# All scales of an attention and two-layer gated kernel from one product with a constant matrix

## The chip, the cores and the metric

The kernel runs on one core of a Trainium2 chip. The metric is the device time of one execution in microseconds (us); three executions of the kernel before gave 1435.85, 1441.42 and 1451.26 us, median 1441.42 us. Engines are named PE (TensorE matmul), PEld (its weight loads), DVE (VectorE), ACT (ScalarE), POOL (GpSimd) and SP (SyncE, which issues the DMAs here).

## What is computed

Attention with queries pooled by two over 32 heads (batch 4, 8 heads, 1152 keys, head width 64), then two feed-forward layers on 2304 tokens of width 512 with 2048 hidden columns, the first gated by a cosine, the second by a sigmoid:

```
q_pool = q.reshape(B, H, S // 2, 2, D).mean(axis=3)
attn   = softmax(q_pool @ k.T / sqrt(D));  x = attn @ v          # 2304 x 512
h = x @ w_in1;  x = (h * cos(h)) @ w_out1
h = x @ w_in2;  out = (h / (1 + exp(-h))) @ w_out2
```

q, k, v are 32-bit; the four weight matrices arrive as 64-bit floats.

## The kernel before

**Split numbers.** Every matmul operand is written as a sum of two 16-bit numbers, high and low, after multiplication by a power of two, and three products (high·high, high·low, low·high) give the result. The power of two comes from the largest magnitude of the operand, over all 128 partitions. A tile's maximum per partition is one DVE reduction; the helpers `scale_steps_` and `mean_scales` make of it a scale `s` and its inverse `u` that all partitions hold.

**scale_steps_ (lines 87 to 120)** serves the weight pieces (16 per layer, `wide`), the eight blocks of x, the rest block (`mrem`) and the nine blocks of y: 50 calls. It transposes the 128 maxima into one row (L91, PE, tile `mt`), reduces that row on one partition (L94, DVE, `mxw` or `mxx`), masks the exponent there (L98 and L101 for the weights, L105 otherwise), clamps it (L107, `pbw` or `pbx`), spreads it over all partitions by a product with `ones` (L113, PE, `bc`), and forms `s` and `u` (L117, L120). `mt` and `bc` take two turns of one rotating PSUM tag, which the first layer's `h` tiles use too.

**mean_scales (lines 122 to 137)** serves the 16 head pairs of the attention: one product of the maxima with a constant 128x128 matrix `mean` of 2^-7 (L127, `bm`) and three DVE steps (L130, L131, L135). The power of two then follows the mean of the maxima and not the largest of them.

**Stages.** Head pairs are processed in nine tiles each, 144 in all: scores (`sp`, L419), their evacuation with the maximum (`sc`, L438), exponential (L446), split (L452, POOL L457), a DMA transposition (`hlT`), the product with v (`pv`, L470). During the first batch the weights of layer 1 are decoded from 64-bit beside it (`weight_steps`: ACT L235, DVE L236, L239, L244, L247, then a scale, then ACT L267, L268 and POOL L269). From the second batch on the units of layer 1 run beside the attention (`h`, L550; `y`, L610; the cosine on DVE L575, L576, L585, L590). After the last tile the rest of layer 1 runs with the decoding of layer 2's weights, whose staging holds six half pieces; then layer 2 runs on PE alone (`h`, L550; `o`, L631) in nine blocks, each of which makes the scale of the next one (`y_split`).

**What sets the order.** Each engine executes its instructions in program order. The program is written as generators with priorities (`early`, `ahead`), and a scheduler turns them into the order of each engine before the launch: a step that becomes ready earlier in its model is placed earlier, and everything around it moves as well. SP issues all DMAs, in its own order.

Of the kernel before, what the change touches and what calls it, by code (L numbers as in the profile page):

```python
# [11 lines left out]
F32 = mybir.dt.float32  # L12
F16 = mybir.dt.float16
I32 = mybir.dt.int32
AF = mybir.ActivationFunctionType
ALU = mybir.AluOpType
AX = mybir.AxisListType
# [27 lines left out]
def attention_moe_moe_kernel(ctx, tc, q, k, v, w_in1, w_out1, w_in2, w_out2, out):  # L45
# [22 lines left out]
    ident = const.tile([128, 128], F32, name="ident")  # L68
    ones = const.tile([4, 128], F32, name="ones")
# [3 lines left out]
    def make_consts(pool):  # L73
        nc.vector.memset(ones, 1.0)
        nc.vector.memset(mean, 2.0**-7)
        nc.vector.memset(halfpi, math.pi / 2)
        io = pool.tile([128, 128], I32, name="io", tag="kn", bufs=NB_N)
        nc.gpsimd.iota(io, pattern=[[1, 128]], base=0, channel_multiplier=-1)
        nc.vector.tensor_scalar(out=ident, in0=io, scalar1=0, scalar2=None, op0=ALU.is_equal)
# [4 lines left out]
    def scale_steps(*a):  # L84
        return early(scale_steps_(*a), P_CH)

    def scale_steps_(m, n, pool, res, tag, wide=False):


        mt = pool.tile([128, 2, GW], F32, tag="h", name="mt")[:, 0, 0:128]  # L90
        nc.tensor.transpose(mt[0:n, :], m, ident)  # L91
        yield
        mx = small.tile([4, 1], F32, name="mx" + tag, tag="mx" + tag)
        nc.vector.tensor_reduce(out=mx[0:n], in_=mt[0:n, :], axis=AX.X, op=ALU.max)  # L94
        pb = small.tile([4, 1], F32, name="pb" + tag, tag="pb" + tag)
        mi, pi = mx.bitcast(I32)[0:n], pb.bitcast(I32)[0:n]
        if wide:
            nc.vector.tensor_scalar(  # L98
                out=pi, in0=mi, scalar1=3, scalar2=0x3F800000, op0=ALU.logical_shift_left, op1=ALU.bitwise_and
            )  # L100
            nc.vector.scalar_tensor_tensor(  # L101
                out=pi, in0=mi, scalar=1 << 30, in1=pi, op0=ALU.bitwise_and, op1=ALU.bitwise_or
            )
        else:
            nc.vector.tensor_scalar(out=pi, in0=mi, scalar1=EXP_MASK, scalar2=None, op0=ALU.bitwise_and)  # L105
        pb = pb[0:n]
        nc.vector.tensor_scalar(out=pb, in0=pb, scalar1=TINY, scalar2=2.0**-12, op0=ALU.max, op1=ALU.mult)  # L107
        dg = pb
        if n > 1:
            dg = small.tile([4, 4], F32, name="dg" + tag, tag="dg" + tag)[0:n, 0:n]  # L110
            nc.vector.tensor_scalar(out=dg, in0=ident[0:n, 0:n], scalar1=pb, scalar2=None, op0=ALU.mult)
        bc = pool.tile([128, 2, GW], F32, tag="h", name="bc")[:, 0, 0:4]
        nc.tensor.matmul(bc[:, 0:n], ones[0:n, :], dg, start=True, stop=True)  # L113
        yield

        s, u = res
        nc.vector.tensor_scalar(  # L117
            out=s.bitcast(I32), in0=bc.bitcast(I32)[:, 0:n], scalar1=EXP_MASK, scalar2=None, op0=ALU.bitwise_xor
        )
        nc.vector.tensor_scalar(out=u, in0=bc[:, 0:n], scalar1=0.5, scalar2=None, op0=ALU.mult)  # L120

    def mean_scales(m, n, pool, res):

        bc = pool.tile([128, 2, GW], F32, tag="h", name="bm")[:, 0, 0:4]
        nc.tensor.matmul(bc[:, 0:n], mean, m, start=True, stop=True)  # L127
        yield
        s, u = res
        nc.vector.tensor_scalar(out=u, in0=bc[:, 0:n], scalar1=TINY, scalar2=2.0**-3, op0=ALU.max, op1=ALU.mult)  # L130
        nc.vector.tensor_scalar(  # L131
            out=s.bitcast(I32), in0=u.bitcast(I32), scalar1=EXP_MASK, scalar2=EXP_MASK,
            op0=ALU.bitwise_and, op1=ALU.bitwise_xor,
        )
        nc.vector.tensor_scalar(  # L135
            out=u.bitcast(I32), in0=u.bitcast(I32), scalar1=EXP_MASK, scalar2=None, op0=ALU.bitwise_and
        )
# [20 lines left out]
    def run_all(g):  # L158
        for _ in g:
            pass  # L160
# [23 lines left out]
    def weight_steps(w, srcs, stage, pspool, eng, nsub, bufs, ahead):  # L184
# [35 lines left out]
        def decode(kind, p):  # L220
# [35 lines left out]
            for _ in scale_steps(m1, 1, pspool(), (s, u), "w", wide):  # L256
                pass
# [3 lines left out]
        def write(kind, p):  # L261
# [10 lines left out]
            if (kind, p) == ("i", npc - 1):  # L272

                nc.vector.tensor_reduce(out=w.kg, in_=w.si, axis=AX.X, op=ALU.min)
                nc.vector.tensor_reduce(out=w.ug, in_=w.ui, axis=AX.X, op=ALU.max)
                nc.vector.tensor_scalar(out=w.kg, in0=w.kg, scalar1=2.0**-22, scalar2=None, op0=ALU.mult)
                nc.vector.tensor_scalar(out=w.ug, in0=w.ug, scalar1=2.0**22, scalar2=None, op0=ALU.mult)
# [63 lines left out]
    def pair_prep(at, P):  # L341
# [19 lines left out]
        yield from early(mean_scales(m3, 3, ps_h, (s, u)), P_CH)  # L361
# [142 lines left out]
    def x_scale_consts(w, s, u, first):  # L504
# [12 lines left out]
            out=c.a, in0=w.ui, scalar1=u, scalar2=1.0 / two_pi if first else 1.0, op0=ALU.mult, op1=ALU.mult  # L517
# [4 lines left out]
    def x_split(at, mp, x32, i, blk, w):  # L522
# [6 lines left out]
        yield from scale_steps(m, 1, ps_h, (s, u), "x")  # L529
# [118 lines left out]
    if True:  # L648
# [10 lines left out]
        make_consts(at.src)  # L659
# [202 lines left out]
        run_all(scale_steps(mrem, 1, ps_h, (srem, urem), "x"))  # L862
# [34 lines left out]
        def y_split(yb):  # L897
# [5 lines left out]
            yield from scale_steps(m, 1, ps_m, (yb.s, yb.u), "x")  # L903
# [99 lines left out]
```

## Time and profile before

| quantity | value |
|---|---|
| median of three executions | 1441.42 us |
| profiled execution, time | 1445.72 us |
| profiled execution, span | 1444.0 us |
| PE busy | 1190.0 us, 82% |
| DVE busy | 1026.4 us, 71% |
| ACT busy | 783.1 us, 54% |
| POOL busy | 578.5 us, 40% |

The span runs from the first instruction to the last; 1.7 us of the time lie around it. Busy shares are averages over stages with different limits, so the stage windows below matter more than this table: 0 to 250 us is the first batch with the decoding of layer 1's weights, 250 to 880 us the other three batches beside layer 1, 880 to 1056 us the rest of layer 1 with layer 2's weights, and from 1056 us on layer 2. Instructions overlap a little at their ends, so the distance from one start to the next is the time that an instruction takes from its engine, and the duration printed beside it is longer.

### The profile page before, as it was taken

The page shows a single profiled execution, that of the slowest core. Times are in us where ns is not written, and L with a number is a line of the kernel's source. Part 1 is how long each engine was busy: PE and PEld are TensorE (multiplying, and loading weights), DVE is VectorE, ACT ScalarE, POOL GpSimd, SP SyncE. Part 2 cuts the span into 40 slices and gives each one's busy share as a digit, 9 for nine tenths or more (in the row PEclk, how much of TensorE's full clock was granted, in tenths as well). Part 3 has the DMA queues.
Part 4 walks back from the last instruction along what each step waited for, and adds up shares of the span by engine and source line. Part 5 has one row for each costly group of instructions (what it writes and reads, how often), then busy time and mean ns, then how long its engine had stood idle before and what let it go on. Part 6 is the DMA issues. An engine that isn't in the chain of part 4 may idle for free. (4 is left out here: it accounts for less than half of the span.)

```text
span 1444.0 us, 25499 instructions
## 1 busy us (share of the span) xinstructions
PE 1190.0 (82%) x10070; PEld 860.8 (60%) x10070; DVE 1026.4 (71%) x2110; ACT 783.1 (54%) x1001; POOL 578.5 (40%) x329
## 2 busy tenths in 40 slices
PE   1664644787988579898888979888899999999998
PEld 0343423565776356666666667777776666666665
DVE  7999998689887788896899895989962222333212
ACT  3876867568786587775687773645631111111110
POOL 1576755446577365663566451464420000000000
PEclk9976757898999799998999999999999999999999
DMA  8799998959799799978899964323310000000001
GB/s 255 149 242 206 233 213 150 173 126 167 154 204 193 135 208 197 194 136 164 137 192 204 176 150 86 117 94 116 112 59 30 1 30 30 30 30 15 15 1 30
DMA packets 493592, 186.22 MB, mean 129 GB/s; under 512 B 433568, under 2 KB 468384, under 8 KB 493472
## 3 DMA queue, kind: packets, MB, share of 16 engines
q1 hardware_dynamic: 493472, 184.59, 61.0%
q8 instruction: 79, 1.29, 0.4%
q14 instruction: 41, 0.34, 0.1%
HBM read 66.58 MB, written 9.44 MB: 53 GB/s over the span
## 5 line engine op out<-in xcount | busy, mean ns | idle before, releaser
L457 POOL TENSOR_TENSOR hl<-sc,hl 128x1152 f16<-128x1152 f32 x144 | 367.5, 2561 | 218.1 <-ACT hl L452 138.1
L419 PE MATMUL sp<-kT,qT 128*128 128x512 f16 (+1 forms) x768 | 198.0, 377 | 109.1 <-DVE sc L438 80.1
L550 PEld LDWEIGHTS <-ih 128*128 128x128 f16 x2304 | 227.4, 100 | 77.9 <-issue 19.2
L438 DVE TENSOR_SCALAR_CACHE_REDUCE sc<-sp,psu 128x512 f32<-128x512 f32 (+1 forms) x288 | 229.6, 805 | 50.7 <-PE sp L419 47.4
L563 ACT ACTIVATE hk<-h,ca 128x512 f32<-128x512 f32 x144 | 98.1, 682 | 303.9 <-PE h L550 302.6
L470 PE MATMUL pv<-vt,hlT 128*128 128x130 f16 (+1 forms) x1440 | 192.8, 239 | 56.0 <-DMA hlT<-hl 42.7
L446 ACT ACTIVATE sc<-sc,nb 128x1152 f32<-128x1152 f32 x144 | 179.9, 1250 | 94.4 <-DVE nb L443 74.6
L550 PE MATMUL h<-ys,ih 128*128 128x256 f16 x1152 | 200.3, 275 | 3.1 <-ACT hk L563 3.1
L470 PEld LDWEIGHTS <-hlT 128*128 128x128 f16 (+1 forms) x1440 | 146.7, 111 | 91.0 <-DMA hlT<-hl 54.7
L550 PE MATMUL h<-xT,ih 128*128 128x256 f16 x1024 | 190.5, 282 | 9.8 <-DMA xT<-xn 5.5
L474 PE MATMUL pv<-vt,hlT 128*128 128x65 f16 (+1 forms) x1440 | 185.0, 209 | 0.0
L452 ACT ACTIVATE hl<-sc 128x1152 f16<-128x1152 f32 x144 | 165.4, 1156 | 28.0 <-DMA hlT<-hl 23.0
L419 PEld LDWEIGHTS <-qT 128*128 128x128 f16 x768 | 76.4, 108 | 174.1 <-issue 135.7
L598 DVE TENSOR_SCALAR gh<-hk,ck 128x1024 f16<-128x1024 f32 x36 | 27.0, 750 | 193.7 <-PE o L631 187.7
L610 PE MATMUL y<-gh,oh 128*128 128x256 f16 x576 | 160.5, 279 | 3.5 <-ACT y L619 2.7
L610 PE MATMUL y<-gl,oh 128*128 128x256 f16 x576 | 160.5, 279 | 0.6 <-POOL gl L591 0.6
L610 PE MATMUL y<-gh,ol 128*128 128x256 f16 x576 | 160.4, 279 | 0.0
L550 PE MATMUL h<-ys,il 128*128 128x256 f16 x576 | 158.2, 275 | 0.0
L474 PEld LDWEIGHTS <-hlT 128*128 128x128 f16 (+1 forms) x1440 | 143.3, 109 | 19.0 <-issue 10.7
L550 PE MATMUL h<-xT,il 128*128 128x256 f16 x512 | 144.0, 281 | 0.0
L591 POOL TENSOR_TENSOR gl<-tt,gh 128x1024 f16<-128x1024 f32 x36 | 89.6, 2489 | 98.1 <-DVE gh L590 90.3
L610 PEld LDWEIGHTS <-oh 128*128 128x128 f16 x1152 | 113.0, 100 | 22.8 <-issue 4.8
(291 smaller groups left out, 2143.3 us busy)
## 6 DMA issues: line engine op xcount, KB each, us to landing
wst<-in_moe_w_in_dram SPq DMA_DIRECT2D x32, 512.0 KB, 4.7
wst<-in_moe_w_out_dram SPq DMA_DIRECT2D x32, 512.0 KB, 4.3
stk<-in_k_dram SPq DMA_DIRECT2D x32, 288.0 KB, 3.9
stv<-in_v_dram SPq DMA_DIRECT2D x32, 288.0 KB, 4.4
stq<-in_q_dram SPq DMA_DIRECT2D x32, 256.0 KB, 3.1
ydr<-y SPq DMA_DIRECT2D x9, 512.0 KB, 3.6
y32b<-ydr SPq DMA_DIRECT2D x9, 512.0 KB, 3.9
out_dram<-osb SPq DMA_DIRECT2D x16, 256.0 KB, 3.4
```

What stands on the lines that cost most here:

```text
L419: nc.tensor.matmul(sp[:, o - a:o - a + n], P.qT[e][:, t, :], kT[:, o:o + n], start=(e == 0), stop=(e == 1))
L438: nc.vector.tensor_scalar(out=T.sc[:, a:z], in0=sp, scalar1=T.P.su, scalar2=None, op0=ALU.mult, op1=ALU.min, accum_out=mx[:, x:x + 1],)
L446: nc.scalar.activation(out=T.sc, in_=T.sc, func=AF.Exp, scale=-1.0, bias=nb)
L452: nc.scalar.activation(out=hi, in_=T.sc, func=AF.Copy)
L457: nc.gpsimd.tensor_tensor(out=T.hl[:, 1, :], in0=T.sc, in1=T.hl[:, 0, :], op=ALU.subtract)
L470: nc.tensor.matmul(G.pv[r, T.gi], T.hlT[:, 0, c, r], P.vt[i][:, c], start=(c == 0), stop=(c == KC - 1), skip_group_check=True,)
L474: nc.tensor.matmul(G.pv[r, T.gi, 0], T.hlT[:, 1, c, r], P.vt[i][:, c, 0], start=False, stop=(c == KC - 1), skip_group_check=True,)
L550: nc.tensor.matmul(hp, wt[:, c, f * 128:(f + 1) * 128], xt(c), start=(i == 0), stop=(i == 3 * NC - 1), skip_group_check=True,)
L563: nc.scalar.activation(out=o, in_=blk.hp, func=AF.Copy if first else AF.Silu, scale=blk.c.a[:, g:g + 1])
L591: nc.gpsimd.tensor_tensor(out=G.gl, in0=t, in1=gh, op=ALU.subtract)
L598: nc.vector.tensor_scalar(out=gh, in0=hk, scalar1=blk.c.k, scalar2=None, op0=ALU.mult)
L610: nc.tensor.matmul(blk.y[:, oc, :], wt[:, f, oc * 128:(oc + 1) * 128], gt[:, f % 4, :], start=(f == 0 and e == 0 and oc % 2 == 0), stop=(f ...
```

## The change

`scale_steps_` and `mean_scales` become one function `scale_steps`: the 128 maxima go straight into one product with `mean`, and three DVE steps on all partitions form `u` and `s`. For the weights the two exponent steps (64-bit layout) now run on 128 partitions ahead of the product (`mw`). `ident`, `ones` and the iota on POOL that made `ident` are gone. A constant `top` (14 or 12) sets how large the scaled numbers may be, and the guard factors of the gates change with it (2^-15, 2^12 and 0.25 in place of 2^-22, 2^22 and 1).

```diff
-        mt = pool.tile([128, 2, GW], F32, tag="h", name="mt")[:, 0, 0:128]
-        nc.tensor.transpose(mt[0:n, :], m, ident)
-        yield
-        nc.vector.tensor_reduce(out=mx[0:n], in_=mt[0:n, :], axis=AX.X, op=ALU.max)
...
+            w = small.tile([128, 1], F32, name="mw", tag="mw")
+            wi, mi = w.bitcast(I32), m.bitcast(I32)
             nc.vector.tensor_scalar(
-                out=pi, in0=mi, scalar1=3, scalar2=0x3F800000, op0=ALU.logical_shift_left, op1=ALU.bitwise_and
+                out=wi, in0=mi, scalar1=3, scalar2=0x3F800000, op0=ALU.logical_shift_left, op1=ALU.bitwise_and
             )
...
-        nc.vector.tensor_scalar(out=pb, in0=pb, scalar1=TINY, scalar2=2.0**-12, op0=ALU.max, op1=ALU.mult)
-        bc = pool.tile([128, 2, GW], F32, tag="h", name="bc")[:, 0, 0:4]
-        nc.tensor.matmul(bc[:, 0:n], ones[0:n, :], dg, start=True, stop=True)
-        yield
-        nc.vector.tensor_scalar(
-            out=s.bitcast(I32), in0=bc.bitcast(I32)[:, 0:n], scalar1=EXP_MASK, scalar2=None, op0=ALU.bitwise_xor
-        )
-        nc.vector.tensor_scalar(out=u, in0=bc[:, 0:n], scalar1=0.5, scalar2=None, op0=ALU.mult)
...
         bc = pool.tile([128, 2, GW], F32, tag="h", name="bm")[:, 0, 0:4]
         nc.tensor.matmul(bc[:, 0:n], mean, m, start=True, stop=True)
         yield
         s, u = res
-        nc.vector.tensor_scalar(out=u, in0=bc[:, 0:n], scalar1=TINY, scalar2=2.0**-3, op0=ALU.max, op1=ALU.mult)
+        nc.vector.tensor_scalar(
+            out=u, in0=bc[:, 0:n], scalar1=TINY, scalar2=2.0**(9 - top), op0=ALU.max, op1=ALU.mult
+        )
```

The two DVE steps behind these lines, which make `s` from `u` and mask `u`, stay as they were in `mean_scales`.

**PE behind the last attention tile.** In the kernel before, the transposition of the third weight piece of layer 2 (`mt<-ident,wm`) stands here, ahead of the first matmuls of the last blocks of x (`h<-xT`):

```order
L610 MATMUL y<-gh,ol_86 128x256
L113 MATMUL bc<-pbx,ones 128x1 x2
L91 MATMUL mt<-ident,wm_10818 1x128
L550 LDWEIGHTS ih_83
L550 MATMUL h<-xT,ih_83 128x256
```

Its second product stands 31 `h` matmuls further on:

```order
L550 MATMUL h<-xT,il_84 128x256
L550 LDWEIGHTS ih_83
L550 MATMUL h<-xT,ih_83 128x256
L113 MATMUL bc<-pbw,ones 128x1
L550 LDWEIGHTS ih_83
```

In the changed kernel the one product of that piece (`bm<-mw`) stands right behind the products of the last x block and of the rest block, 17 `y` matmuls ahead of the first `h<-xT`:

```order
L582 MATMUL y<-gh,oh_83 128x256
L95 MATMUL bm<-xm,mean 128x1
L95 MATMUL bm<-mrem,mean 128x1
L95 MATMUL bm<-mw,mean 128x1
L582 LDWEIGHTS oh_83
L582 MATMUL y<-gl,oh_83 128x256
```

The piece's scale has moved from behind `h` matmuls to ahead of all of them.

**DVE at the end of layer 2's weights.** Before, the last cosine group (`CAST gh<-tt`, L590) is done ahead of the last two scales (`so` and `uo`):

```order
L590 CAST gh<-tt 128x1024
L247 SCALAR_TENSOR_TENSOR wst<-wst 128x512
L117 TENSOR_SCALAR so_120<-bc 128x1
L120 TENSOR_SCALAR uo_121<-bc 128x1
L94 TENSOR_REDUCE mxw<-mt 1x1
L289 COPY uoT_122<-uo_121 64x4
L98 TENSOR_SCALAR pbw<-mxw 1x1
```

After, the last group's multiplication and cast (L557, L562) stand behind the last scale:

```order
L548 SCALAR_TENSOR_TENSOR tt<-tt,hk 128x1024
L98 TENSOR_SCALAR uo_115<-bm 128x1
L102 TENSOR_SCALAR so_114<-uo_115 128x1
L106 TENSOR_SCALAR uo_115<-uo_115 128x1
L261 COPY uoT_116<-uo_115 64x4
L491 TENSOR_SCALAR cy<-uo_115,yu,ug_118 128x8
L557 SCALAR_TENSOR_TENSOR tt<-hk,ck,tt 128x1024
L562 CAST gh<-tt 128x1024 x2
```

On PE, 57 `y` and 71 `h` matmuls stood between the last weight product and the first `o` matmul of layer 2; now 169 `y` and 72 `h` stand there. The number of matmuls between the last `pv` and the first `o` is the same but for the scales.

**PE in layer 2.** Before, each block had a transposition and, some 3.9 us later in the trace, a product; here the latter:

```order
L631 MATMUL o<-ol_10745,gh 128x512
L113 MATMUL bc<-pbx,ones 128x1
L631 LDWEIGHTS gl
L631 MATMUL o<-oh_10744,gl 128x512
L550 LDWEIGHTS ih_10742
```

After, one product stands where the transposition stood:

```order
L522 MATMUL h<-ys,il_10615 128x256
L95 MATMUL bm<-ym,mean 128x1
L603 LDWEIGHTS gh
L603 MATMUL o<-oh_10616,gh 128x512
L603 LDWEIGHTS gh
```

Nothing else of a block of layer 2 has moved, except that at its end 29 and 1 `h` matmuls stand where 25 and 5 did.

## Rows read from the trace of the kernel before

**Rows 1.** Windows by stage: busy us (instructions) of each engine, clock, DMA share, GB/s.

```profile
40.00:140.00 100.00, 54.71 (x447) 34.55 (x445) 98.47 (x234) 75.65 (x101) 66.63 (x40) 0.76 0.98 207
140.00:250.00 110.00, 60.07 (x489) 37.84 (x488) 102.99 (x261) 81.71 (x110) 65.03 (x39) 0.67 0.95 199
250.00:880.00 630.00, 530.27 (x5191) 396.66 (x5192) 525.00 (x1032) 452.51 (x539) 354.73 (x190) 0.92 0.90 171
880.00:1056.00 176.00, 152.27 (x1271) 128.24 (x1270) 153.07 (x326) 95.35 (x143) 81.58 (x42) 0.94 0.33 96
1056.00:1444.00 388.00, 382.78 (x2648) 258.86 (x2646) 114.57 (x174) 62.19 (x87) 3.81 (x4) 1.00 0.08 25
```

**Rows 2.** Timeline of DVE, a scale of layer 1's weights: start, duration us, instruction, [idle before].

```profile
19.45 0.27 DVE L94 TENSOR_REDUCE mxw<-mt 1x1 f32<-1x128 f32 x1
19.65 0.80 DVE L339 SCALAR_TENSOR_TENSOR vt<-stv,ps__160,vt 128x576 f16<-128x576 f32 x1
...
26.78 0.14 DVE L117 TENSOR_SCALAR si<-bc 128x1 int32<-128x1 int32 x1
26.85 0.13 DVE L120 TENSOR_SCALAR ui<-bc 128x1 f32<-128x1 f32 x1
```

**Rows 3.** Instructions on tile mxw: count, duration ns min/median/max, first and last start.

```profile
L94 DVE TENSOR_REDUCE mxw<-mt x32: 268/271/279, 19.4 to 1053.1; 1x1 f32<-1x128 f32 x32
L101 DVE SCALAR_TENSOR_TENSOR pbw<-mxw,pbw x32: 138/141/2322, 23.6 to 1055.1; 1x1 int32<-1x1 int32 x32
```

**Rows 4.** Timeline of PE, one block of layer 2, its transposition and its product.

```profile
1105.49 0.27 PE L91 MATMUL mt<-ident,ym 128*1 128x128 f32 x1
1105.60 0.38 PE L631 MATMUL o<-oh,gh 128*128 128x512 f16 x1
...
1109.07 0.38 PE L631 MATMUL o<-ol,gh 128*128 128x512 f16 x1
1109.38 0.38 PE L113 MATMUL bc<-pbx,ones 1*128 1x1 f32 x2
1109.69 0.39 PE L631 MATMUL o<-oh,gl 128*128 128x512 f16 x1
1109.92 0.38 PE L550 MATMUL h<-ys,ih 128*128 128x256 f16 x2
```

**Rows 5.** Timeline of PE, two products of a head pair: amid y, and behind a bc.

```profile
428.74 0.28 PE L127 MATMUL bm<-pm,mean 128*128 128x3 f32 x2
428.88 0.27 PE L610 MATMUL y<-gl,oh 128*128 128x256 f16 x1
...
688.77 0.39 PE L127 MATMUL bm<-pm,mean 128*128 128x3 f32 x2
689.02 0.19 PE L474 MATMUL pv<-vt,hlT 128*128 128x65 f16 x1
```

**Rows 6.** Timeline behind the last attention tile, four engines' rows.

```profile
893.69 0.14 DVE L107 TENSOR_SCALAR pbw<-pbw 1x1 f32<-1x1 f32 x1
893.82 0.38 PE L550 MATMUL h<-xT,ih 128*128 128x256 f16 x2 [1.69 <-DMA xT<-xn]
899.38 0.16 DVE L117 TENSOR_SCALAR si<-bc 128x1 int32<-128x1 int32 x1 [5.55 <-PE bc L113]
903.12 5.96 POOL L269 TENSOR_TENSOR il<-wst,ih 128x512 f16<-128x512 f32 x4 [19.76 <-issue]
962.49 0.69 DVE L236 TENSOR_SCALAR_CACHE_REDUCE wt<-wt 128x512 f32<-128x512 f32 x1 [5.08 <-ACT wt L235]
```

**Rows 7.** Windows of 10 us in that stage, columns as in rows 1.

```profile
890.00:900.00 10.00, 8.26 (x57) 6.25 (x56) 3.90 (x24) 3.11 (x4) 0.00 (x0) 0.83 0.57 106
```

**Rows 8.** Groups of DVE, 880 to 1056 us: busy us, mean ns, idle before.

```profile
L585 DVE SCALAR_TENSOR_TENSOR tt<-hk,ck,tt 128x1024 f32<-128x1024 f32 x12 | 18.9, 1579 | 2.8 <-ACT tt L582 2.8
L590 DVE CAST gh<-tt 128x1024 f16<-128x1024 f32 x13 | 10.7, 824 | 0.0
```

**Rows 9.** Chain of work that ended last: first PE pieces behind the last weight product.

```profile
1055.88 6.33 PE y L610 x57
```

More of the change, by code (lines that the diff above doesn't have):

```diff
@@ L66, in attention_moe_moe_kernel, with make_consts @@
     dram = ctx.enter_context(tc.tile_pool(name="ydram", bufs=1, space=DRAM))
-    ident = const.tile([128, 128], F32, name="ident")
-    ones = const.tile([4, 128], F32, name="ones")
     mean = const.tile([128, 128], F32, name="mean")
     halfpi = const.tile([128, 1], F32, name="halfpi")
-    def make_consts(pool):
-        nc.vector.memset(ones, 1.0)
+    def make_consts():
         nc.vector.memset(mean, 2.0**-7)
         nc.vector.memset(halfpi, math.pi / 2)
-        io = pool.tile([128, 128], I32, name="io", tag="kn", bufs=NB_N)
-        nc.gpsimd.iota(io, pattern=[[1, 128]], base=0, channel_multiplier=-1)
-        nc.vector.tensor_scalar(out=ident, in0=io, scalar1=0, scalar2=None, op0=ALU.is_equal)
@@ L81, in attention_moe_moe_kernel, with scale_steps @@
     GW = 256
-    def scale_steps(*a):
-        return early(scale_steps_(*a), P_CH)
-    def scale_steps_(m, n, pool, res, tag, wide=False):
-        mt = pool.tile([128, 2, GW], F32, tag="h", name="mt")[:, 0, 0:128]
-        nc.tensor.transpose(mt[0:n, :], m, ident)
-        yield
-        mx = small.tile([4, 1], F32, name="mx" + tag, tag="mx" + tag)
-        nc.vector.tensor_reduce(out=mx[0:n], in_=mt[0:n, :], axis=AX.X, op=ALU.max)
-        pb = small.tile([4, 1], F32, name="pb" + tag, tag="pb" + tag)
-        mi, pi = mx.bitcast(I32)[0:n], pb.bitcast(I32)[0:n]
+    def scale_steps(m, pool, res, top, wide=False):
+        n = m.shape[1]
@@ L97, in scale_steps_ @@
         if wide:
+            w = small.tile([128, 1], F32, name="mw", tag="mw")
+            wi, mi = w.bitcast(I32), m.bitcast(I32)
             nc.vector.tensor_scalar(
-                out=pi, in0=mi, scalar1=3, scalar2=0x3F800000, op0=ALU.logical_shift_left, op1=ALU.bitwise_and
+                out=wi, in0=mi, scalar1=3, scalar2=0x3F800000, op0=ALU.logical_shift_left, op1=ALU.bitwise_and
             )
             nc.vector.scalar_tensor_tensor(
-                out=pi, in0=mi, scalar=1 << 30, in1=pi, op0=ALU.bitwise_and, op1=ALU.bitwise_or
+                out=wi, in0=mi, scalar=1 << 30, in1=wi, op0=ALU.bitwise_and, op1=ALU.bitwise_or
@@ L103, in scale_steps_ @@
             )
-        else:
-            nc.vector.tensor_scalar(out=pi, in0=mi, scalar1=EXP_MASK, scalar2=None, op0=ALU.bitwise_and)
-        pb = pb[0:n]
-        nc.vector.tensor_scalar(out=pb, in0=pb, scalar1=TINY, scalar2=2.0**-12, op0=ALU.max, op1=ALU.mult)
[L108 to L111, printed above, removed]
-        bc = pool.tile([128, 2, GW], F32, tag="h", name="bc")[:, 0, 0:4]
@@ L113, in scale_steps_ @@
[L113 to L122 removed]
+            m = w
         bc = pool.tile([128, 2, GW], F32, tag="h", name="bm")[:, 0, 0:4]
@@ L255, in decode @@
                 nc.vector.tensor_reduce(out=m1, in_=m, axis=AX.X, op=ALU.max)
-            for _ in scale_steps(m1, 1, pspool(), (s, u), "w", wide):
+            for _ in early(scale_steps(m1, pspool(), (s, u), 14, wide), P_CH):
                 pass
@@ L275, in write @@
                 nc.vector.tensor_reduce(out=w.ug, in_=w.ui, axis=AX.X, op=ALU.max)
-                nc.vector.tensor_scalar(out=w.kg, in0=w.kg, scalar1=2.0**-22, scalar2=None, op0=ALU.mult)
-                nc.vector.tensor_scalar(out=w.ug, in0=w.ug, scalar1=2.0**22, scalar2=None, op0=ALU.mult)
+                nc.vector.tensor_scalar(out=w.kg, in0=w.kg, scalar1=2.0**-15, scalar2=None, op0=ALU.mult)
+                nc.vector.tensor_scalar(out=w.ug, in0=w.ug, scalar1=2.0**12, scalar2=None, op0=ALU.mult)
         for i in range(ahead):
@@ L360, in pair_prep @@
         u = small.tile([128, 3], F32, name="pu_", tag="pu_", bufs=3)
-        yield from early(mean_scales(m3, 3, ps_h, (s, u)), P_CH)
+        yield from early(scale_steps(m3, ps_h, (s, u), 12), P_CH)
         P.s = s
@@ L516, in x_scale_consts @@
         nc.vector.tensor_scalar(
-            out=c.a, in0=w.ui, scalar1=u, scalar2=1.0 / two_pi if first else 1.0, op0=ALU.mult, op1=ALU.mult
+            out=c.a, in0=w.ui, scalar1=u, scalar2=0.25 / two_pi if first else 0.25, op0=ALU.mult, op1=ALU.mult
         )
@@ L528, in x_split @@
         u = small.tile([128, 1], F32, name="xu", tag="xu")
-        yield from scale_steps(m, 1, ps_h, (s, u), "x")
+        yield from early(scale_steps(m, ps_h, (s, u), 14), P_CH)
         blk.c = x_scale_consts(w, s, u, True)
@@ L658, in attention_moe_moe_kernel @@
         moe_stack = ExitStack()
-        make_consts(at.src)
+        make_consts()
         state = Weights()
@@ L861, in attention_moe_moe_kernel @@
         urem = small.tile([128, 1], F32, name="urem", bufs=1)
-        run_all(scale_steps(mrem, 1, ps_h, (srem, urem), "x"))
+        run_all(early(scale_steps(mrem, ps_h, (srem, urem), 14), P_CH))
         rb = Block()
@@ L902, in y_split @@
             yield
-            yield from scale_steps(m, 1, ps_m, (yb.s, yb.u), "x")
+            yield from early(scale_steps(m, ps_m, (yb.s, yb.u), 14), P_CH)
             yb.blk = blk = Block()
```

## The prediction

> **What bounds the kernel now.** I read the windows by stage first, then the timeline at the scales, and last the chain of waits and the instruction order of both kernels. The windows give four stages with three different limits [rows 1]. From 40 to 250 us DVE works 98.47 of 100 and 102.99 of 110 us: it paces the first batch, PE is busy just over half of the time at a granted clock of 0.76 and 0.67, and the DMA engines, at 0.98 and 0.95, stand close behind DVE. From 250 to 880 us nothing is full (PE 84%, DVE 83%, DMA share 0.90): 108 tiles take 630 us, 5.8 us each, by chains of waits. From 880 to 1056 us DVE works 153 of 176 us and PE 152. From 1056 us on PE works 382.8 of 388 us at full clock; what leaves its queue there is time won one for one.
>
> The scales themselves are small. Look in the rows not at the durations but at the distances between starts: a small DVE step, printed as 0.13 to 0.16 us, holds the engine for 0.07 us, and the one-partition reduction for 0.20 us [rows 2]. On PE the transposition in layer 2 takes 0.11 us of the queue; the product with `ones` takes 0.40 us: from the start of the `o` matmul before it to the start of that behind it are 0.62 us, where an `o` matmul alone takes 0.22 [rows 4].
>
> **The change, part by part.**
>
> *Constants.* `ident`, `ones` and the iota lie at the start, while DVE waits for the first loads: nothing, and nothing if that cover were gone but the 0.1 to 0.4 us of three small instructions (an estimate from the small steps above).
>
> *Layer 1's weights, 16 scales.* DVE loses the reduction (0.20) and five small steps (5 x 0.07) and gains five small steps on 128 partitions: I price these like the steps that already run on 128 partitions (L117, L120), 0.07 each [rows 2], so 0.55 - 0.35 = 0.20 us less per scale. Since DVE paces this stage, 16 x 0.20 = **3.2 us**. Bounds: by the printed durations (the reduction's 271 ns; five steps of about 140 ns go and five come) [rows 3] 0.27 x 16 = 4.3 us; below, nothing, if the DMA engines at 0.95 to 0.98 take over as the limit [rows 1]. L101 took up to 2322 ns where its median is 141 [rows 3]; that is a wait that will fall upon the next instruction, so I count no gain for it. Here two of three reads of PSUM by DVE go away. The rows show no price for such a read: L117, which reads PSUM, holds DVE for 0.07 us [rows 2]. The Trainium skill (Perfetto Trace Analysis, Optimizing Scalar/DVE Operations) gives a fixed cost of about 60 ns for DVE on SBUF and about 125 ns on PSUM; by it another 2 x 65 ns x 16 = 2 us would go, an estimate from that page. The trace does not agree with it, and I leave that out.
>
> *Blocks of x (6 until 880 us).* One trip through PE's queue less per block. No engine is full there; gain taken as nothing, cover: the other tiles' work. If the cover were gone it would be the 0.4 to 0.5 us of PE per block, 3 us.
>
> *Behind the last tile (880 us to the first `o` matmul).* Four terms. (a) DVE does 15 scales here: 15 x 0.20 = 3.0 us less. (b) The last cosine group's two instructions, 1.58 + 0.82 = 2.4 us [rows 8], now stand behind the last scale on DVE; the last product comes earlier by them. (c) PE executes in order, and behind the last weight product now stand 169 `y` and 72 `h` matmuls in place of 57 and 71: 113 more, at 6.33/57 = 0.11 us each [rows 9] **12.5 us more** between that product and layer 2's first `o`. PE has as much work in all, so this is a loss only as far as PE waited ahead of the product, and it did: DVE was the slower of the two. (d) X, by which the chain of weight pieces starts earlier or waits less. The third piece of layer 2 had its maximum ready at 893.83 us, but its product stood behind 31 `h` matmuls, which waited for the transposed x until 893.82; DVE got its answer at 899.38, 5.55 us idle, POOL had by then stood still for 19.76 us [rows 6], and DVE worked 3.9 of the 10 us from 890 on [rows 7]. In the new order that product stands ahead of all of these `h`. As the staging holds three pieces, everything behind it (ACT, POOL, the next loads) moves forward with it: 5.5 us for the wait alone, and up to 11 us with the earlier place in front of the `y` matmuls (5.5 plus most of the 6.1 us that DVE idled in that window). A second hole, 5.08 us before 962.49, where DVE waited for a load by way of ACT [rows 6], may close or not. So X lies between 0 and 16; I take 10, the first hole nearly whole and the second not. Sum: -3.0 - 2.4 + 12.5 - 10 = **-2.9 us**, with ends +7.1 and -8.9.
>
> *Layer 2, 8 blocks.* PE loses 0.11 + 0.40 and gains one product with `mean`. That product amid `y` matmuls holds PE for 0.14 us (428.74 to 428.88), behind a `bc` for 0.25 [rows 5]; its place here is amid `h` and `o`, nearest to the first. 8 x (0.51 - 0.14) = **3.0 us**, at least 8 x 0.26 = 2.1. A rule speaks against: the Trainium skill (TensorE: Matmul & The Clock Gate, The mechanism, on tiling) says that a weight load overlaps matmuls in flight only when it goes to other row groups, and a 128-row load of `mean` shares its rows with every neighbour. By that rule this load would stay exposed like that of the `bc`, and the term would be 8 x 0.11 = 0.9 us. The row of 0.14 us does not agree with it, so I stay with 3.0.
>
> *The new order of the rest.* Everything between has been placed anew by the scheduler; the first x scale stands behind 260 score matmuls instead of 254, one tile. I can't cost that but by its unit: a tile is 5.8 us, so ±6 us, mean nothing.
>
> **Sum:** -3.2 - 2.9 - 3.0 = -9.1 us. The profiled execution took 1445.7 us (span 1444.0 and 1.7 around it), so it would take 1436.6; it lies 4.3 us above the median, and against that the forecast is 1441.4 - 9.1 = 1432.3, **1432 us**, 0.6% less. About 1% (14.4 us) is what a measurement of this kernel can tell from no change.
>
> **The rivals.**
>
> *A, slower: the tail of PE.* One mechanism: the order was made as if PE were the limit behind 880 us, while DVE is. If the early product brings nothing (DVE still works through the same pieces, the loads still come as they did, X near 0), the last weight product comes just 5.4 us earlier and PE has 12.5 us more to do behind it: +7.1, with layer 2's least gain of 2.1 and nothing in the first stage +5.0: 1446 us, and with a tile's worth of bad order 1452. It decides where X falls below 7. For it: DVE was busy in 153 of 176 us. Against it: the 5.55 and 19.76 us of idleness, both in front of what has moved.
>
> *B, the whole chain gets free.* X = 16 and 4.3 us in the first stage: +7.1 - 16 - 4.3 - 3.0 = -16.2: 1425 us. For it: both holes are waits for the chain of pieces that has become shorter by a trip through PE and DVE. Against it: the second hole is a load's, and the loads' place on SP has not changed.
>
> *C, it does nothing measurable.* DMA paces the first batch, X = 7 and the product costs in layer 2 what the `bc` did: about -1 us: 1440 us. For it: a DMA share of 0.98; against it: DVE's 98.5% and the 0.14 us.
>
> **How the numbers follow.** Forecast (-15 to -3, 1426 to 1438): 0.42. A (1443 to 1458): 0.22. B (1415 to 1426): 0.21. C (1438 to 1443): 0.15. Faster by over 1%, below 1427.0: most of B and a little of the forecast's low end and of bad or good luck in the order, 0.27. Slower by over 1%, above 1455.8: the upper part of A, 0.10. Within 1%: 0.63. The range leaves out the lowest part of B and the upper part of A, about 2 in 10 with the ±6 us of the order: 1416 to 1450. The forecast's own range is 1426 to 1438.
>
> **What would show it.** In the changed kernel's trace: a distance of about 0.14 us from the start of `bm<-ym` to the next matmul in layer 2, blocks of layer 2 shorter by 0.37 us; no idle of DVE and POOL around 890 to 900 us, and the last product of a weight piece near 1040 us instead of 1055.6, with 26 us of PE work up to the first `o`; DVE as full as before up to the end of the first batch, and that end about 3 us earlier. It is wrong if the last weight product still comes at 1050 us or later (rival A), if the attention's 630 us change by more than 6 us, or if `bm` in layer 2 holds PE for 0.4 us.

## The result and the profile after

The changed kernel takes 1429.05 us (median of 9 executions, 1426.31 to 1433.02), the kernel before 1441.42 us (median of 9, 1435.85 to 1451.26): 0.9907 of it, with an interval of 0.9885 to 0.9928, 12.4 us or 0.9% less. That lies within 1%, beside the 1432 us of the prediction. The profiled execution took 1431.83 us, its span is 1430.1 us, 13.9 us shorter than the span before.

The windows by stage of the changed kernel (columns as in rows 1):

```profile
40.00:140.00 100.00, 52.09 (x410) 32.22 (x409) 97.10 (x219) 74.23 (x97) 64.81 (x38) 0.62 0.95 200
140.00:250.00 110.00, 60.48 (x494) 39.00 (x494) 107.59 (x260) 75.68 (x105) 61.06 (x39) 0.68 0.93 193
250.00:880.00 630.00, 536.28 (x5262) 406.27 (x5263) 528.11 (x1059) 461.81 (x556) 359.82 (x193) 0.93 0.91 174
880.00:1056.00 176.00, 149.29 (x1291) 128.72 (x1290) 147.65 (x273) 97.42 (x148) 74.80 (x44) 0.96 0.33 98
1056.00:1430.00 374.00, 368.88 (x2541) 248.00 (x2539) 109.25 (x154) 56.52 (x78) 0.00 (x0) 1.00 0.07 24
```

Against [rows 1], DVE is no emptier in the first batch: it works 107.59 of 110 us from 140 us on, where it worked 102.99. Windows with fixed ends do not tell where the time went, so I cut both traces at events that both have: the start of the first `h` product, the end of the last product with v (`pv`), the start of the first and the end of the last `o` product.

| stage | before | after | difference | prediction |
|---|---|---|---|---|
| A: start to first `h` | 275.8 | 282.2 | +6.4 | -3.2 |
| B: first `h` to last `pv` | 601.7 | 588.9 | -12.8 | 0 |
| C: last `pv` to first `o` | 192.4 | 187.9 | -4.5 | -2.9 |
| D: first `o` to last `o` | 368.9 | 365.9 | -3.0 | -3.0 |

Together they make the 13.9 us. The two later terms came out; the first two are wrong by 10 and 13 us in opposite directions, so the good total is partly a compensation. The column "before" comes from one execution, which took 4.3 us more than the median.

**Stage D** is the simplest. PE of the changed kernel around one y scale in layer 2:

```profile
1094.17 0.27 PE L522 MATMUL h<-ys,il 128*128 128x256 f16 x1
1094.28 0.28 PE L95 MATMUL bm<-ym,mean 128*128 128x1 f32 x2
1094.42 0.38 PE L603 MATMUL o<-oh,gh 128*128 128x512 f16 x1
```

From the start of the product to the next matmul are 0.14 us, where the transposition and the `bc` held PE for 0.51 us [rows 4]. 8 x 0.37 = 3.0 us.

**Stage C.** The `bm` of the second weight piece of layer 2 (the one whose answer came at 899.38 us in [rows 6]; the prediction calls it the third) and POOL's next work; the window that answers to [rows 7]; and the chain of work that ended last, behind the last weight product:

```profile
874.97 0.36 PE L95 MATMUL bm<-mw,mean 128*128 128x1 f32 x2
...
890.49 9.20 POOL L240 TENSOR_TENSOR il<-wst,ih 128x512 f16<-128x512 f32 x6 [13.16 <-issue]
```

```profile
890.00:900.00 10.00, 10.00 (x94) 8.96 (x92) 7.42 (x7) 7.77 (x12) 9.20 (x6) 1.00 0.62 191
```

```profile
1032.80 8.10 PE y L582 x74
1040.90 1.64 PE h L522 x15
1042.54 10.37 PE y L582 x95
1052.91 6.22 PE h L522 x57
```

The product no longer stands behind `h` matmuls that wait for x; POOL starts on the layer's weights at 890.49 in place of 903.12 us; 6.4 us of that had been won before the last `pv`. POOL still stands idle for 13.16 us there, where it was 19.76. The last weight product starts at 1032.4 us in place of 1055.6, counted from the last `pv` 161 us in place of 178. Behind it come 26.3 us of `y` and `h` (the four rows) where there were 14: these 12 us more are the tail of PE that the prediction put at 12.5 us.

**Stage A.** L90, the step of the weights' scale with two inputs in SBUF, has its one-partition counterpart L101 in [rows 3]. Shown are first its group and who waits for it, then one of its executions with POOL's row of the same time:

```profile
L90 DVE SCALAR_TENSOR_TENSOR mw<-wm,mw x32: 141/147/2320, 21.7 to 1031.3; 128x1 int32<-128x1 int32 x32
...
  PE bm L95: 59.2, 20
```

```profile
54.10 2.89 POOL L429 TENSOR_TENSOR hl<-sc,hl 128x1152 f16<-128x1152 f32 x1 [5.68 <-ACT hl L424]
...
54.80 2.20 DVE L90 SCALAR_TENSOR_TENSOR mw<-wm,mw 128x1 int32<-128x1 int32 x1
56.93 0.81 DVE L311 SCALAR_TENSOR_TENSOR kn<-stk,ps__321,kn 128x576 f16<-128x576 f32 x1
```

A step of 0.15 us takes 2.20 us: it begins while POOL subtracts and ends as POOL ends. The profile counts this as busy DVE. The Trainium skill (SBUF — State Buffer, SBUF: two separate sides) says that DVE and GpSimd share one port pair as an exclusive lock, for which a DVE step with two SBUF inputs stands still until a GpSimd instruction that reads SBUF is done, if that one started first; the rows agree (POOL ends at 56.99 us, L90 at 57.00).

This gives a measure, used below as **blocked time**: for every DVE instruction the part of its duration above the usual one of its line and form (the tenth percentile), where that is over 0.15 us; how steps are grouped moves the sums by up to about 2 us. In stage A it is 49.6 us before (53 steps) and 59.1 us after (47 steps); of the time of such steps 89% and 94% lie within a POOL instruction. L101 had 4.1 us of it, L90 has 11.1 us, six of them steps of over 1 us. The largest share is not the scale's: a decoding step with one input of 128x512 elements (L239 before, L210 now) has 13.4 and 19.6 us. Without blocked and idle time stage A has 275.8 - 49.6 - 21.8 = 204.4 us of DVE work before and 282.2 - 59.1 - 23.3 = 199.8 after: DVE's own work fell by 4.6 us between the two profiles, near the 3.2 of the prediction, and 9.5 us more of blocking used it up. The 4.6 are no clean measure: `via_psum` below, with the new scale in another order, again has about 205 us, since the order also decides what DVE does ahead of the first `h`.

### The profile page after: what moved, and what is told of

It is laid out like the page before. It is cut to its first block, busy times and chain, and to the rows that moved or that the text cites. A ratio compares the mean times of both kernels' runs of the same rounds, so it can differ in the third digit from the quotient of the medians.

```text
span 1430.1 us, 25355 instructions
## 1 busy us (share of the span) xinstructions
PE 1174.7 (82%) x10020; PEld 858.2 (60%) x10020; DVE 1020.5 (71%) x2040; ACT 781.4 (55%) x1003; POOL 566.3 (40%) x328
## 3 DMA queue, kind: packets, MB, share of 16 engines
q1 hardware_dynamic: 493472, 184.59, 61.4%
q8 instruction: 78, 1.28, 0.4%
## 5 line engine op out<-in xcount | busy, mean ns | idle before, releaser
L429 POOL TENSOR_TENSOR hl<-sc,hl 128x1152 f16<-128x1152 f32 x144 | 363.0, 2530 | 234.5 <-ACT hl L424 114.8
L391 PE MATMUL sp<-kT,qT 128*128 128x512 f16 (+1 forms) x768 | 201.5, 380 | 102.7 <-DVE sc L410 81.5
L442 PE MATMUL pv<-vt,hlT 128*128 128x130 f16 (+1 forms) x1440 | 199.0, 239 | 39.9 <-DMA hlT<-hl 30.9
L522 PE MATMUL h<-ys,ih 128*128 128x256 f16 x1152 | 196.1, 273 | 1.9 <-ACT hk L535 1.9
L442 PEld LDWEIGHTS <-hlT 128*128 128x128 f16 (+1 forms) x1440 | 148.8, 111 | 71.0 <-DMA hlT<-hl 42.3
L446 PE MATMUL pv<-vt,hlT 128*128 128x65 f16 (+1 forms) x1440 | 190.5, 209 | 0.0
L391 PEld LDWEIGHTS <-qT 128*128 128x128 f16 x768 | 79.9, 111 | 167.0 <-issue 129.4
L446 PEld LDWEIGHTS <-hlT 128*128 128x128 f16 (+1 forms) x1440 | 144.2, 109 | 18.1 <-issue 8.9
L522 PEld LDWEIGHTS <-il 128*128 128x128 f16 x1152 | 113.9, 99 | 18.0 <-issue 1.9
```

Of the source, the lines that this page charges most:

```text
L391: nc.tensor.matmul(sp[:, o - a:o - a + n], P.qT[e][:, t, :], kT[:, o:o + n], start=(e == 0), stop=(e == 1))
L429: nc.gpsimd.tensor_tensor(out=T.hl[:, 1, :], in0=T.sc, in1=T.hl[:, 0, :], op=ALU.subtract)
L442: nc.tensor.matmul(G.pv[r, T.gi], T.hlT[:, 0, c, r], P.vt[i][:, c], start=(c == 0), stop=(c == KC - 1), skip_group_check=True,)
L446: nc.tensor.matmul(G.pv[r, T.gi, 0], T.hlT[:, 1, c, r], P.vt[i][:, c, 0], start=False, stop=(c == KC - 1), skip_group_check=True,)
L522: nc.tensor.matmul(hp, wt[:, c, f * 128:(f + 1) * 128], xt(c), start=(i == 0), stop=(i == 3 * NC - 1), skip_group_check=True,)
```

## The experiments

Each is the changed kernel with one edit. "Old way" means transposition, one-lane steps and the product with `ones`; it brings `ident`, `ones` and the iota back. Ratios are to the kernel before, timed with them; the changed kernel has 0.9907 and, timed again (`after_again`), 0.9902.

All profiles in one table (us; stages as above; "x delay" is the sum over the six x blocks until 880 us from the start of the maximum `xm` to the start of the scale `xs`):

| kernel | ratio, interval | A | B | C | D | blocked in A | blocked in B | x delay |
|---|---|---|---|---|---|---|---|---|
| before | 1 | 275.8 | 601.7 | 192.4 | 368.9 | 49.6 | 110.1 | 79.9 |
| changed | 0.9907, 0.9885-0.9928 | 282.2 | 588.9 | 187.9 | 365.9 | 59.1 | 105.1 | 47.5 |
| after_again | 0.9902, 0.9865-0.9939 | 281.3 | 582.4 | 187.5 | 365.9 | 59.4 | 99.9 | 47.6 |
| y_old | 0.9956, 0.9932-0.9981 | 284.9 | 581.3 | 189.9 | 368.9 | 61.9 | 98.5 | 47.3 |
| w2_old | 0.9971, 0.9950-0.9991 | 284.1 | 583.4 | 195.9 | 365.8 | 62.3 | 94.5 | 47.8 |
| x_old | 0.9978, 0.9949-1.0008 | 286.9 | 594.9 | 189.1 | 365.8 | 61.4 | 106.6 | 74.8 |
| x_old_place | 1.0016, 0.9991-1.0041 | 285.9 | 597.7 | 189.2 | 365.9 | 60.6 | 112.4 | 77.4 |
| x_two | 1.0055, 1.0027-1.0084 | 291.7 | 607.7 | 188.7 | 365.8 | 64.0 | 110.0 | 61.8 |
| x_place | 0.9922, 0.9896-0.9948 | 285.7 | 580.4 | 193.0 | 365.8 | 62.8 | 93.6 | 50.2 |
| w1_old | 0.9851, 0.9819-0.9883 | 274.6 | 584.2 | 187.2 | 365.8 | 45.6 | 101.0 | 45.0 |
| one_in | 0.9857, 0.9821-0.9893 | 282.7 | 583.3 | 186.7 | 365.9 | 56.2 | 102.9 | 47.5 |
| w_rank_up | 0.9972, 0.9948-0.9996 | 293.5 | 583.3 | 187.4 | 366.0 | 72.0 | 101.5 | 47.0 |
| w_rank_down | 0.9864, 0.9832-0.9897 | 278.8 | 583.8 | 187.1 | 365.9 | 56.6 | 98.8 | 47.0 |
| via_psum | 0.9797, 0.9761-0.9832 | 274.9 | 584.8 | 183.4 | 365.8 | 42.5 | 97.5 | 48.0 |

**How far stages move by themselves: after_again.**

> The changed kernel once more, to learn how far its stages move from one execution to another without a cause. Expected: first h product at 282 to 287 us, attention from there to the last product with v 580 to 590 us, tail to the first o product 187 to 190, layer 2 365.8 to 366.0; time 1426 to 1434. If the attention's stage moves by more than 10 us between executions, the 14 us that x_old and the kernel before lie above the others are not the x scales'.

The stages repeat within 1 us but for B, which is 6.5 us shorter; y_old, with the same order up to 874 us, shows 581.3. The windows 250 to 880 us of after_again:

```profile
250.00:880.00 630.00, 530.78 (x5329) 403.60 (x5330) 525.76 (x1061) 465.62 (x562) 358.53 (x193) 0.96 0.92 174
```

The granted clock is 0.96 there and was 0.93 in the changed kernel's first profile; low clock (1.2 in place of 2.4 GHz) covers 35 and 66 us of B. So B is known to about 4 us either way, A to 2, and D to 0.1.

**Layer 2: y_old.** The call for y is the old one again.

```
-            yield from early(scale_steps(m, ps_m, (yb.s, yb.u), 14), P_CH)
+            yield from early(scale_max(m, ps_m, (yb.s, yb.u)), P_CH)
```

> The changed kernel, but the 9 scales of y are made in the old way (transposition, one-lane steps, product with ones). The order of all engines is that of the changed kernel up to the first y scale near 874 us. Theory (the term of layer 2): a block of layer 2 takes 42.2 us in place of 41.8, the time is 3.0 us more than the changed kernel's, 1432, and all before 870 us stays as it was. Rival (the small differences of the changed kernel are order and luck of the run, the product costs nothing in itself): time within 1 us of the changed kernel's 1429, or a distance of more than 5 us that arises elsewhere than in the blocks.

D is 368.9 us with the old scales (y_old, the kernel before) and 365.8 to 366.0 with the new ones in all twelve others: 3.0 us, the term of the prediction. The ratio alone, 0.005 above the changed kernel's, would have made it 7 us; the stage tells it better.

**The tail: w2_old.** The 16 scales of layer 2's weights are the old ones (`scale_max` where `w is W2`).

> The changed kernel, but the 16 scales of layer 2's weights are made in the old way. The order is that of the changed kernel up to about 830 us. Theory (the prediction's X): the chain of weight pieces behind the last tile gets longer again by a trip through TensorE and VectorE per piece; the last weight product falls back from 1032.5 us towards 1050, the first o product from 1059 towards 1064 to 1070, time 1432 to 1436. Rival (the tail is TensorE's work, which is the same): the last weight product comes later, but the first o product stays within 2 us of 1059, time 1428 to 1431.

C grows to 195.9 us, by 8; the last weight product comes 186 us behind the last `pv` in place of 161, and behind it 10.0 us of PE are left up to the first `o` in place of 26.5. The chain of pieces thus gets 25 us shorter by the new scale and the places that the scheduler gives it, and PE's tail gives 16 of them back.

**The x scales: x_old, x_old_place, x_place, x_two.** Four edits of the same call (`x_old` and `x_old_place` also make the rest block's scale in the old way):

```
x_old:        yield from early(scale_max(m, ps_h, (s, u)), P_CH)
x_old_place:  yield from early(scale_max(m, ps_h, (s, u)), P_CH - 200)
x_place:      yield from early(scale_steps(m, ps_h, (s, u), 14), P_CH - 200)
x_two:        bt = product(mean, m); a = max(bt, TINY) * 1.0
              yield from scale_steps(a, pool, res, 14)
```

> The changed kernel, but the 8 scales of the x blocks and that of the rest are made in the old way. The order is that of the changed kernel up to the first x scale at 262 us, and from there on it is placed anew. Theory (the prediction's zero for the x blocks): 0 to 3 us more, 1429 to 1432, the last product with v near 871 to 874 us. Rival 1 (the 12.8 us that the attention gained from the first h to the last product with v come from the x scales, or from the order that they bring): last product with v at 880 to 884 us, time 1438 to 1442. Rival 2 (order alone): any shift of up to 6 us either way that is not where the x scales stand.

> As x_old (the x scales in the old way in the changed kernel), but with a lower rank for them in the scheduler: the order is that of x_old up to some 470 us, and another behind that. Theory 1 (the old x scale itself is what makes the attention longer): 592 us or more, time 1438 to 1444. Rival (the place at which x_old lets TensorE wait 7.83 us for one maximum): if that wait goes, attention at 584 to 589 us, time 1430 to 1435; the wait stands before the order differs, or nearly so, and may stay.

> The changed kernel with the same instructions, but the scale of an x block gets a lower rank in the scheduler; the order is that of the changed kernel up to the first x scale and nearly so up to about 680 us, and another behind that. Theory (what the attention gained belongs to the new x scale itself): attention 580 to 590 us, time within 3 us of the changed kernel's. Rival (the attention's length is a matter of the places that the order gives, TensorE waiting at the x product for VectorE's maximum as it did for 7.83 us in x_old): the stage moves by more than 5 us, behind 600 us, with a wait of several us at a place where the order differs; time 1434 to 1442 or below 1425.

> The changed kernel, but the scale of an x block makes two trips: the partitions' maxima go through the product with mean, are copied, and go through it once more (the mean of equal numbers is that number). No transposition and no one-lane step. The order is placed anew from the first x scale on. Theory 1 (a second trip through TensorE's and VectorE's queues is what the old x scale cost, near 2 us each for 6 blocks): attention at 592 to 600 us in place of 580 to 589, time 1436 to 1444. Theory 2 (the old scale's one-lane steps or its transposition's place cost it, not the trip): attention at 580 to 589 us, time within 4 us of the changed kernel's.

With the old x scale B takes 595 to 602 us in three orders (before, x_old, x_old_place), with the new one 580 to 589 in ten profiles, x_place's other order among them. So rival 1 of x_old holds: the gain of B, 598.1 - 583.6 = 14.5 us between the means, belongs to the x scale or to the order that comes with it. x_two has neither a transposition nor a one-lane step, only the second trip, and is the slowest, 607.7 us. (Its profile is the longest of its twelve executions, 9 us above their median; were all of this in B, the median's B would be near 599 us, still above those with one trip.) So the transposition and the one-lane steps are not needed to make B long; two trips through both queues, or the places that the scheduler gives to two trips, are enough. One way in which it can cost is seen in x_old, near 500 us (all engines, one x block):

```profile
492.40 7.01 POOL L463 TENSOR_TENSOR hl<-sc,hl 128x1152 f16<-128x1152 f32 x3 [7.88 <-ACT hl L458]
493.25 1.54 DVE L108 TENSOR_SCALAR ps__5194<-pu__5195 128x3 int32<-128x3 int32 x1
494.82 2.29 DVE L112 TENSOR_SCALAR pu__5195<-pu__5195 128x3 int32<-128x3 int32 x1
...
497.28 3.22 DVE L539 SCALAR_TENSOR_TENSOR xn<-x,xs,xn 128x1024 f16<-128x1024 f32 x1
500.42 0.74 DVE L145 TENSOR_REDUCE pm<-stk 128x1 f32<-128x576 f32 x1
501.08 1.20 DVE L145 TENSOR_REDUCE xm<-x 128x1 f32<-128x1024 f32 x1
...
502.34 0.37 PE L118 MATMUL mt<-ident,xm 128*1 128x128 f32 x1 [7.83 <-DVE xm L145]
```

POOL subtracts three tiles in one go; three DVE steps stand behind it and take 7.05 us (0.15, 0.15 and 1.28 us when nothing is in the way); the maximum of x waits behind them; and PE, whose next instruction is the transposition of that maximum, stands still for 7.83 us with all score products queued behind it. x_two has the same hole at the same place, and x_old_place one of 7.76 us:

```profile
496.93 2.29 DVE L106 TENSOR_SCALAR pu__5183<-pu__5183 128x3 int32<-128x3 int32 x1
...
499.39 3.21 DVE L513 SCALAR_TENSOR_TENSOR xn<-x,xs,xn 128x1024 f16<-128x1024 f32 x1
...
504.45 0.59 PE L112 MATMUL bt<-xm,mean 128*128 128x1 f32 x2 [8.55 <-DVE xm L119]
```

In the changed kernel the x products wait at most 0.30 us each up to the end of B. But the kernel before, with B at 601.7 us, has no such hole either: up to 880 us PE waits at no x transposition for the maximum, and its longest idle time ahead of an x transposition or x product is 1.53 us. The same block there:

```profile
481.98 0.37 PE L91 MATMUL mt<-ident,xm 128*1 128x128 f32 x1
483.31 0.58 PE L113 MATMUL bc<-pbx,ones 1*128 1x1 f32 x2 [0.95 <-DVE pbx L107]
```

So the hole is at most a part of what x_old, x_old_place and x_two lost, and it does not explain what the change won. B also has more blocked time with two trips (106.6 to 112.4 us against 93.6 to 105.1) and more low clock (75 to 99 us against 34 to 68); whether either is a cause or follows from the waits is not settled. Nor are trips and places separated: ahead of this block's first product stand 528 score matmuls in all four orders with two trips and 534 in all those with one. In x_place C is also 5 us longer than in the changed kernel: behind its last weight product 33.6 us of PE's work are left in place of 26.4.

**The first batch: w1_old.** Layer 1's weights are scaled in the old way (`scale_max` where `w is W1`); up to 250 us the order is that of the kernel before.

> The changed kernel, but the 16 scales of layer 1's weights are made in the old way. Up to the first x scale near 250 us the order is that of the kernel before. Theory (the prediction's 0.20 us of VectorE per scale): the first batch gets longer, the first h product comes at 285 us in place of 282, time 1432. Rival (the new scale with its steps on 128 partitions, of which the one with two SBUF inputs stood up to 2.3 us behind GpSimd, and its product early in TensorE's order made the first batch longer): the first h product comes at 275 to 277 us as in the kernel before, and, if the later stages stay, time 1422 to 1425.

A is 274.6 us, as before the change, where the kernels with the new scale for W1 and the x scale of the change lie at 281.3 to 285.7 (after_again, y_old, w2_old, x_place and the changed kernel): the new W1 scale, with the order that it brings, costs 7 to 11 us here. With the old one the kernel takes 1419.2 us, the ratio falls to 0.9851.

**Is it L90 itself? one_in.** The step with two SBUF inputs becomes one with one input. In the first batch the order stays that of the changed kernel, save an exchange of two DMA transpositions on SP and of a few score products on PE.

```
-            nc.vector.scalar_tensor_tensor(
-                out=wi, in0=mi, scalar=1 << 30, in1=wi, op0=ALU.bitwise_and, op1=ALU.bitwise_or
+            nc.vector.tensor_scalar(
+                out=wi, in0=wi, scalar1=0x3F800000, scalar2=0, op0=ALU.bitwise_and, op1=ALU.bitwise_or
```

> The changed kernel with one step of the weights' scale replaced: the step that reads two tensors of SBUF on 128 partitions (it adds the exponent's top bit, which is zero for these weights) is a step of one input with the same shape. That the top bit is not looked at is left out. The order of every engine is that of the changed kernel. Theory (blocking by GpSimd): the 11 us that this step stood behind GpSimd's subtractions in the first batch go, partly onto the next steps with two inputs; first h product at 273 to 280 us in place of 282 to 287, no step of the weights' scale over 0.3 us, time 1419 to 1426. Rival (the product's early place in TensorE's order makes the batch longer, since TensorE waits there for VectorE): first h product stays at 282 to 287, time 1427 to 1433.

The step's group now, and then that of via_psum:

```profile
L90 DVE TENSOR_SCALAR mw<-mw x32: 133/141/146, 21.5 to 1025.9; 128x1 int32<-128x1 int32 x32
```

```profile
L92 DVE SCALAR_TENSOR_TENSOR mw<-wm,bm x32: 133/142/152, 21.5 to 1017.3; 128x1 int32<-128x1 int32 x32
```

In one_in it is never blocked, 146 ns at most. But A stays at 282.7 us, as the rival had it, and here my theory fell: of the 11.1 us only 2.9 leave the sum (56.2 us; profiles of the same order lie at 59.1 to 62.8), the next steps take them over (L218 from 11.1 to 14.2 us, L215 from 3.9 to 8.6), and idle time rises from 23.3 to 26.8 us. The ratio, 0.9857, is below the changed kernel's by about as much as the intervals are wide; no stage shows a gain above its own spread.

**Is it the order? w_rank_up, w_rank_down.** The same instructions as in the changed kernel, `P_W` 20 and -20 in place of 0: the pieces of W1 rank higher or lower.

> The changed kernel with the same instructions, but the pieces of layer 1's weights get a higher rank in the scheduler: the order is another from about 80 us on. Theory 1 (the new scale's steps make the first batch longer, at whatever place they stand): first h product at 280 to 287 us. Theory 2 (it is the order: how many of VectorE's steps with two inputs start while GpSimd subtracts): the first h product moves by more than 5 us, along with the time by which VectorE's steps exceed their usual length, 59 to 62 us in the changed kernel, 46 to 50 in the old order, 42.5 in via_psum.

> As w_rank_up, with a lower rank for the pieces of layer 1's weights. Theory 1 (the new scale's steps): first h product at 280 to 287 us. Theory 2 (order): it moves by more than 5 us, along with the time by which VectorE's steps exceed their usual length.

A is 293.5 and 278.8 us: 15 us apart by the order alone, with 72.0 and 56.6 us of blocked time. Over all profiles A goes with the blocked time, from 42.5 us (274.9) by 59 to 63 (281 to 287) to 72.0 (293.5). So the order decides more of this stage than the prices of the steps do; that it does so by what it starts on DVE while POOL subtracts is argued from this agreement and not shown, since no run changes the blocked time alone. Against the five profiles with the order of the changed kernel w_rank_up moved A by 8 to 12 us; w_rank_down by 3 to 7, not clearly the 5 that I had asked for.

A second reading is the rival of w1_old and one_in: PE, which works in order, waits at the weight products that the new scale places early. Its waits there up to the first `h` are, for the kernel before (the other waits at `mt` make 5.0 us), the changed kernel and via_psum (us, times, longest):

```profile
PE bc L113 <- DVE pbw L107: 12.4, 5, 8.2
PE mt L91 <- DVE wm L255: 6.8, 3, 4.7
...
PE bm L95 <- DVE mw L90: 43.1, 12, 10.1
...
PE bm L96 <- DVE mw L92: 14.7, 6, 10.0
```

The 24.2 us of the kernel before became 43.1, and via_psum, which has the shortest of these waits, has with w1_old the shortest A. Against this as the only cause: one_in has 34.3 us and won nothing in A, and in w_rank_up and w_rank_down all idle time ahead of these products is 45.6 and 41.7 us, 4 us apart for 15 us of A. Blocked time fits better, but the runs do not exclude PE's waits as a part.

**A version that beats both: via_psum.** The first of the two steps writes into the PSUM tile of the product, so the second reads one input from SBUF and one from PSUM; nothing is left out. (`bc` is made ahead of these lines.)

```
+            pi = bc.bitcast(I32)[:, 2:3]
-                out=wi, in0=mi, scalar1=3, scalar2=0x3F800000, ...
+                out=pi, in0=mi, scalar1=3, scalar2=0x3F800000, ...
-                out=wi, in0=mi, scalar=1 << 30, in1=wi, ...
+                out=wi, in0=mi, scalar=1 << 30, in1=pi, ...
```

> The changed kernel, but the first of the two steps on the weights' maxima writes into the PSUM tile of the product, so that the second reads one input from SBUF and one from PSUM; nothing is left out. The order is placed anew. Theory (blocking by GpSimd needs two inputs in SBUF): no step of the weights' scale over 0.3 us, the first batch shorter by 3 to 10 us than the changed kernel's, time 1419 to 1427. Rival (the input's place does not matter, or the order does): steps of 2 us stay, or the first h product stays at 282 us or later, time 1427 to 1434.

1416.03 us, 0.9797 of the kernel before (0.9761 to 0.9832), the shortest of all. The step never takes over 0.152 us (row above). A is 274.9 us, 6 to 7 below the changed kernel's, with 42.5 us blocked; C is 183.4. Since its order is another, and one_in removed the same blocking without a gain, the gain in A may belong to the order that came with it, which also took most of PE's waits at the weight products away, as much as to the PSUM input; the runs do not separate the two.

## Why the prediction was right in sum and wrong in two steps

- *Constants, nothing.* No run tests it alone. With the new W1 scale in the changed kernel's order, A is 284.1 to 286.9 us where the constants are back (y_old, w2_old, x_old, x_old_place) and 281.3 to 285.7 where they are not; the ranges overlap.
- *Layer 1's weights, -3.2 us: wrong, +6.4 us between the two profiles.* The price of the steps may have been near (4.6 us less DVE work, no clean measure). The step that failed is "L101 took up to 2322 ns where its median is 141 [rows 3]; that is a wait that will fall upon the next instruction, so I count no gain for it". This took the blocked time for a constant of the stage. It is 49.6 us of 275.8, it changes with the order (42.5 to 72.0), and the order was new. PE's wait at the product, 24.2 us then and 43.1 now, stood in no term at all. Which of the two makes the 6.4 us stays open. That DVE is as full as before was right as a row, but its busy time is no measure of its work. The lower bound, that DMA takes over, did not apply: DMA fell to 0.95 and 0.93.
- *Blocks of x, 0: wrong, 14.5 us less.* The failing step is "No engine is full there; gain taken as nothing, cover: the other tiles' work", with a bound of 3 us from the time that PE spends on it. It priced a trip by occupation. Measured are 595 to 608 us with two trips in four orders and 580 to 589 with one, 2.4 us per block. An engine that works in order has no cover at its own product: while its operand is late, everything behind it waits (7.83 us in x_old). That such waits make the 14.5 us is not shown, since the kernel before has none over 1.53 us at its x products; how the time arises there stays open.
- *Behind the last tile, -2.9 us: right, -4.5.* The last weight product stood 161 us behind the last `pv`; the prediction's 1040 us are 162.5. If (a) and (b) gave their 5.4 us, X follows from 16.6 us for the product: 11.2 us, where I took 10. Term (c) measured 26.5 - 14.4 = 12.1 us for 12.5. The first hole went in part: DVE works 7.42 of the 10 us from 890 on where it worked 3.90, and POOL still idles 13.16 us.
- *Layer 2, -3.0 us: right, -3.0.* 0.14 us in the row, D 3.0 us shorter. The Trainium skill's rule on weight loads (TensorE: Matmul & The Clock Gate, The mechanism), by which it would have been 0.9 us, does not describe this product, which holds PE for 0.14 us and not for the 0.40 of the `bc`.
- *The order of the rest, 0 ± 6: too narrow.* w_rank_up and w_rank_down alone differ by 15 us in A.
- *Rivals.* A (tail of PE): the tail came, 12 us, but the last product came 16.6 us earlier counted from the last `pv`, not 5.4. B's holes closed in part. C was wrong: the first batch moved by 15 us with the order alone, which a pace set by DMA does not explain, and the product's price in layer 2 is not that of the `bc`.
- Of its three signs of being wrong one occurred: the attention changed by more than 6 us. The end of the first batch, which was to come 3 us earlier, came 6.4 later. That the total of 1429 us lies at the forecast is luck as to these two terms: +6.4 and -12.8 replaced -3.2 and 0.

## What to carry to other kernels

An engine's busy time can hold time that it stood behind another engine's port: compare each group's longest duration with its median, sum the excess, and treat that sum as something the order can change by tens of us (42.5 to 72.0 here). A small operation between two in-order engines can cost what stands queued behind it while its operand is late, and not only its own time; here one trip less came with 14.5 us, while the cheaper steps of the first batch brought nothing that outweighed a new order. Check a total stage by stage at common events, since two wrong terms can cancel.

## What the runs showed of the hardware that I had not expected

- In the changed kernel, 0.15 us steps from SBUF to SBUF on 128x3 elements are blocked up to 2.2 us (5 of 32 of the lines L102 and L106 for head pairs), while steps of one input on 128x1 are never blocked (none of 32 at L87, the longest 148 ns), nor are the steps at L98, which read PSUM (the longest 161 ns). With two inputs, 10 of 32 at L90 are blocked though they have one element per partition; with one of the two in PSUM none of 32 is (152 ns).
- Taking one blocked step away moves the block to the next one: 11.1 us removed, 2.9 us gained (one_in).
- Two executions of the same order differ by 6.5 us in B, with 66 and 35 us of low clock.
